# Issuing the value loads of a decode attention kernel from ScalarE's DMA queue

## The chip, the cores and the metric

The kernel runs on one core of one Trainium2 chip. A core has five engines that run their own instruction streams: TensorE (PE in the profile), VectorE (DVE), ScalarE (ACT), GpSimd (POOL) and SyncE (SP). Work moves between HBM and the on-chip memory on 16 DMA engines; SP and ScalarE each have a DMA queue of their own, which the profile calls q1 and q10. The metric is the device time of one execution in microseconds.

## The reference, cut to what matters

One token (a row of 448) goes through a block of grouped-query attention over a long cache and, beside it, a small mixer MLP; a gate mixes the two.

```python
q = x @ wq                                  # 16 query heads of 256
k, v = repeat(k_cache, 2), repeat(v_cache, 2)   # 8 heads x 65536 rows x 256, bf16
p = softmax(q k^T / 16)
a = (p v) @ wo
b = mixer_mlp(layernorm(x))                 # 448 x 1792, elementwise in S = 1
g = sigmoid(sum(x * gate_w))
out = g * a + (1 - g) * b
```

Nearly all of the work is reading the two caches once: 8 heads x 65536 rows x 256 values of two bytes, twice.

## The kernel before, in words

The cache is cut into 32 loads (NP) of keys and 32 of values, four of each (PPH) to a head. A load is 128 partitions x 128 rows (NV) of 256 bf16 values: 8 MB, of which each partition gets 64 KB in one piece. The 32 iterations follow the loads.

Keys live in a ring of 192 slots (`kring`), one and a half loads long. Values live in one buffer of 128 slots (`vbuf`), exactly one load: the next values can be fetched only when the last value matrix multiplication on the present ones has ended.

What each engine does in iteration j:

- TensorE (the loop from L531): `keys` transposes the eight chunks of key load j into PSUM (L355) and multiplies them with the queries (L376). Four chunks lie in the first half of the load, four in the second. Then `values` multiplies the probabilities with the values in `vbuf` (L407, 128 of them) and signals `sem_pv`. From iteration 3 on (LEAD is 2) the values lag the keys by one load: iteration j consumes key load j and value load j-1. At the start of the next iteration comes `maxima` (L393, L395), two small steps that VectorE needs for the running maximum of load j. At the end of a head (every fourth iteration) TensorE also projects the finished head (L457, L468).
- VectorE (the loop with `evacuate`, L675): copies half of the transposed chunks out of PSUM, computes the running maximum (`maxima`, L681 to L704), and in iterations 4 to 17 a step of the mixer MLP (`mixer`, L650 to L668), whose middle, a tanh, is on ScalarE.
- ScalarE (the loop with L820): copies the other half of the chunks, then `weights` computes the probabilities of this load (L803 and L807, after a wait for VectorE's maximum), and in iterations 4 to 17 (MIX0 is 4, 14 steps) the mixer's tanh (L825, after a wait for VectorE). Before its loop it issues six small loads (L780 to L785).
- SP (L256 to L319) does nothing but issue DMAs, in an order written out by hand, each behind the wait that makes its buffer free. Key load j goes out when the first half of load j-1 has been transposed (`sem_tr`); key loads 0, 2, 3 and 31 go out in halves or smaller parts. Behind it, after a wait on `sem_pv`, goes value load j-1 (`load_v`, L271 to L281), and at a head's end the next slice of the projection matrix `wo` (L259). The last value load, 31, goes out in five pieces after the loop, the first of them into the key ring.

All these loads stand in SP's one queue, so they are carried out in the order of issue.

Of the kernel before, what the change touches and what calls it, by code (L numbers as in the profile page):

```python
# [12 lines left out]
def bass_gated_mix__gqa_block_cached__mixer_token_mlp__decode_kernel(  # L13
# [25 lines left out]
    P = 128  # L39
# [11 lines left out]
    NV = BODY * NT  # L51
    NP = NC // BODY
    PPH = NCPH // BODY
# [9 lines left out]
    LEAD = 2  # L63
# [32 lines left out]
    with ctx:  # L96
        def sb(shape, dt, name):
            return ctx.enter_context(nc.sbuf_tensor(name, shape, dt))
# [4 lines left out]
        def new_sem(name):  # L103
            return ctx.enter_context(nc.semaphore(name))
# [3 lines left out]
        vbuf = sb([P, NV, DH], bf16, "vbuf")  # L108
# [91 lines left out]
        sem_v = new_sem("sem_v")  # L200
# [11 lines left out]
        sem_pv = new_sem("sem_pv")  # L212
# [8 lines left out]
        s_hb = new_sem("s_hb")  # L221
# [11 lines left out]
        s_q = new_sem("s_q")  # L233
# [16 lines left out]
        def src(cache, j, n0=0, n1=NV):  # L250
            g, m = divmod(j, PPH)
            s = cache[0, g, m * BODY * CH:(m + 1) * BODY * CH, :].rearrange("(p n) d -> p n d", p=P)
            return s[:, n0:n1, :].rearrange("p n d -> p (n d)")

        @block.sync
        def _(eng):  # L256
            def load_wo(g):
                w = A_wo[g * REP * DH:(g + 1) * REP * DH, :]
                eng.dma_start(wo_rows, w.rearrange("(p i) n -> p (i n)", i=2 * REP)).then_inc(sem_wo, 16)  # L259

            load_wo(0)
            eng.dma_start(wq_s.rearrange("p u n -> p (u n)"),
                          A_wq.rearrange("r n -> (r n)").rearrange("(p m) -> p m", p=P)).then_inc(sem_wq, 16)
            def load(dst, cache, j, n0, n1, at, sem):
                eng.dma_start(dst[:, at + n0:at + n1, :].rearrange("p n d -> p (n d)"), src(cache, j, n0, n1)
                              ).then_inc(sem, 16)

            load(kring, A_k_cache, 0, HV, NV, 0, sem_k)
            load(kring, A_k_cache, 0, 0, HV, 0, sem_kb)

            def load_v(j):  # L271
                if j == 0:
                    eng.wait_ge(s_q, 1)
                    eng.wait_ge(s_hb, 1)
                else:
                    eng.wait_ge(sem_pv, j)
                load(vbuf, A_v_cache, j, 0, NV, 0, sem_v)
                g, m = divmod(j, PPH)
                if m == 0 and 1 <= g < H - 1:
                    eng.wait_ge(s_proj, g)  # L280
                    load_wo(g)  # L281

            for j in range(NP):
                if j == LEAD + 1:
                    eng.wait_ge(sem_tr[NB - 1], BODY * LEAD)
                    load(kring, A_k_cache, j, HV, NV, HV, sem_kc[1])
                    eng.wait_ge(sem_tr[NB - 1], BODY * LEAD + DC // 2)
                    load(kring, A_k_cache, j, 0, HV // 2, HV, sem_kq[0])
                if j >= 1:
                    eng.wait_ge(sem_tr[NB - 1], BODY * (j - 1) + DC)  # L290
                if j == LEAD:
                    load(kring, A_k_cache, j, HV, NV, 0, sem_k)
                    load(kring, A_k_cache, j, 0, HV, 0, sem_kc[0])
                elif j == LEAD + 1:
                    load(kring, A_k_cache, j, HV // 2, HV, HV, sem_kq[1])
                elif j == NP - 1:
                    load(kring, A_k_cache, j, 0, HV, HV, sem_k)
                    load(kring, A_k_cache, j, HV, NV, HV, sem_kc[2])
                elif j >= 1:
                    load(kring, A_k_cache, j, 0, NV, HV * (j % 2), sem_k)  # L300
                if j < LEAD:
                    load_v(j)
                elif j > LEAD:
                    load_v(j - 1)


            for (n0, n1), sem in zip(pieces, sem_vp):
                if n0 == 0:
                    eng.wait_ge(sem_tr[NB - 1], BODY * (NP - 1) + DC)
                elif n0 == NRING:  # L310
                    eng.wait_ge(sem_pv, NP - 1)
                load(kring if n1 <= NRING else vbuf, A_v_cache, NP - 1, n0, n1, 0, sem)
            eng.wait_ge(s_proj, H - 1)
            for h in range(REP):
                w = A_wo[(HQ - REP + h) * DH:(HQ - REP + h + 1) * DH, :]
                eng.dma_start(wo_sb[:, h, :], w.rearrange("(p j) n -> p (j n)", j=2)).then_inc(sem_wl[h], 16)
            eng.wait_ge(s_fin, NCG)
            eng.dma_start(out_ap, out_row[:, :]).then_inc(sem_out, 16)
            eng.wait_ge(sem_out, 16)  # L319
# [16 lines left out]
        def _(pe):  # L336
# [95 lines left out]
            def piece_wait(n):  # L432
                for (n0, _), sem in zip(pieces, sem_vp):
                    if n == n0:
                        pe.wait_ge(sem, 16)
# [342 lines left out]
        @block.scalar  # L778
        def _(act):
            act.dma_start(xrow_b, x_row_ap).then_inc(sem_x, 16)  # L780
            act.dma_start(grow_b, gate_w.rearrange("(a n) -> a n", a=1)).then_inc(sem_misc, 16)
            for i, w in enumerate((B_w1.rearrange("a f -> (a f)"), B_b1, B_w2.rearrange("f a -> (f a)"))):
                act.dma_start(wrows_b[i * FT:(i + 1) * FT, :], w.rearrange("(k p) -> k p", p=P)
                              ).then_inc(sem_misc, 16)
            act.dma_start(b2_b[:, :], B_b2.rearrange("(a n) -> a n", a=1)).then_inc(sem_misc, 16)  # L785
            act.sem_inc(sem_exp, 1)
            for b in range(1, NB, 2):
                act.sem_inc(sem_ev[b], 1)
            act.wait_ge(s_d2a, 1)
            act.sqrt(statb[:, 3:4], statb[:, 2:3])  # L790
            act.activation(statb[:, 5:6], statb[:, 4:5], AF.Exp, scale=-1.0).then_inc(s_a2d, 1)

            act.wait_ge(s_q, 1)
            act.activation(qrow[:, 1, :], kst[:, 1, :], AF.Copy).then_inc(s_qc, 1)

            pt_reg = act.alloc_register("pt_reg")
            act.reg_mov(pt_reg, DC)
            mix_reg = act.alloc_register("mix_reg")
            act.reg_mov(mix_reg, 1)

            def weights(j1):
                act.wait_ge(s_mneg, j1)
                act.activation(fade[:, :], mdif[:, :], AF.Exp, scale=scale).then_inc(s_fade, 1)  # L803
                for half in range(2):
                    p0 = act.snap(pt_reg, min_val=0, max_val=DC)
                    for hh in range(REP):
                        ins = act.activation(pT[:, bass.ds(p0, DC), hh:2 * NT:REP],  # L807
                                             scores_all.rearrange("p (a r n hh) -> p a hh r n", a=2, r=DC, hh=REP)[:, half, hh],
                                             AF.Exp, bias=mneg[:, hh:hh + 1], scale=scale)
                    if half == 0:  # L810
                        act.reg_sub(pt_reg, DC, pt_reg)
                ins.then_inc(sem_exp, 1)

            with nc.Fori(0, NP, 1, engines=OrderedEngineSet([act.engine])) as j:
                c0 = act.snap(j * BODY, min_val=0, max_val=NC)
                for k in range(BODY):
                    act.wait_ge(sem_qk, c0 + (k + 1))
                    for b in range(1, NB, 2):
                        act.wait_ge(sem_tr[b], c0 + (k + 1))
                        act.activation(ktT[:, k % KTB, b, :], kst_b[:, b, :], AF.Copy).then_inc(sem_ev[b], 1)  # L820
                weights(act.snap(j + 1, min_val=1, max_val=NP))
                with act.If(j >= MIX0):
                    with act.If(j < MIX0 + FT):
                        act.wait_ge(s_u, act.snap(mix_reg, min_val=1, max_val=FT))
                        act.activation(z_b[:, :], z_b[:, :], AF.Tanh).then_inc(s_tanh, 1)  # L825
                        act.reg_add(mix_reg, mix_reg, 1)
            act.wait_ge(s_proj, H)
            for q in range(1, NCG, 2):
                act.activation(out_row[:, q * WG:(q + 1) * WG], prj[32 * q:32 * q + 1, 0:WG], AF.Copy
                               ).then_inc(s_fin, 1)  # L830
# [28 lines left out]
```

## Time and profile before

| | us |
|---|---|
| median of 3 runs | 1264.16 |
| lowest and highest run | 1264.0 and 1265.95 |
| span of the profiled execution | 1262.9 |
| TensorE busy | 964.6 |
| ScalarE busy | 544.5 |
| VectorE busy | 500.2 |

The profile is one execution on the chip. Its page gives the span, busy times by engine, the span in 40 slices, the DMA queues and the costliest groups of instructions. Further views come from the same trace: waits (who waited for whom), the chain of work that ended last, and timelines of one engine in a window. A row of a timeline is: start in us, duration in us, engine and line, operation, output and input with shapes, the number of instructions merged into the row, and in brackets how long the engine was idle before it and what released it. A q after an engine's name means its sequencer, which issues DMAs and is not counted as busy. A row of waits is: who waited for what, us in total, how often, the longest.

### The profile page before, as it was taken

Reading aid. Unit: us, or ns where it says so; the run is one execution under the profiler, and the core shown is the slowest. Engines: PE = TensorE matmul, PEld = TensorE weight load, DVE = VectorE, ACT = ScalarE, POOL = GpSimd, SP = SyncE. Lnnn points to the kernel's source line nnn. Section 1 sums busy time; section 2 is a strip of 40 time slices with the busy share of each in tenths; the row PEclk is TensorE's granted clock in tenths of the full one; section 3 lists DMA queues with packets and bytes.
Section 4 is the critical chain, followed back from the end, with each engine's and each line's share of the span. In section 5 each row is a group of like instructions: output and inputs, shape, how many; then the busy total and the mean of one; then the engine's idle time right before and its main releaser. Section 6 shows DMA issues by size and latency. Waiting matters only on the chain.

```text
span 1262.9 us, 39617 instructions
## 1 busy us (share of the span) xinstructions
PE 964.6 (76%) x17024; PEld 881.7 (70%) x17024; DVE 500.2 (40%) x1128; ACT 544.5 (43%) x692; POOL 0.9 (0%) x7
## 2 busy tenths in 40 slices
PE   4768877688777797767878678876679867698786
PEld 3667876678766687666777667776678756687674
DVE  4334434444544435444444433343333423334342
ACT  2444543345533445333554334443344533345451
POOL 0000000000000000000000000000000000000000
PEclk8779887888878888888987879888798878888897
DMA  9999999999999999999999999999999999999998
GB/s 417 431 421 426 449 432 432 430 432 444 432 434 430 434 432 432 432 434 436 436 434 428 439 432 432 432 440 432 434 432 434 428 440 436 434 432 434 423 438 365
DMA packets 12053, 544.35 MB, mean 431 GB/s; under 512 B 1417, under 2 KB 1676, under 8 KB 2828
## 3 DMA queue, kind: packets, MB, share of 16 engines
q1 hardware_dynamic: 11954, 544.22, 99.7%
q8 instruction: 6, 0.10, 0.0%
q10 hardware_dynamic: 90, 0.01, 0.0%
q14 instruction: 3, 0.02, 0.0%
HBM read 544.22 MB, written 0.00 MB: 431 GB/s over the span
## 4 chain that ended last, share of the span: by engine, by line
DMA 60%; PE 36%; issue 2%; DVE 2%; DVEq 0%; ACT 0%; SPq 0%
DMA kring<-in_A_k_cache_dram 57%; PE kst L355 26%; PE sps L376 6%; DMA vbuf<-in_A_v_cache_dram 3%; PE acc L407 3%; PE acc L457 0%; PE prj L468 0%; PE sps L395 0%; DVE ktT L675 0%; DVE accs L709 0%; PE acc L400 0%; ACT z_b L825 0%; PE sps L393 0%; DVE mrow L686 0%; DVE z_b L656 0%
## 5 line engine op out<-in xcount | busy, mean ns | idle before, releaser
L355 PE MATMUL kst<-ident,kring 128*128 128x128 f32 x4096 | 556.9, 296 | 189.5 <-DMA kring<-in_A_k_cache_dram 166.6
L820 ACT ACTIVATE ktT<-kst 128x1024 bf16<-128x1024 bf16 x512 | 498.6, 1021 | 338.7 <-PE kst L355 338.3
L355 PEld LDWEIGHTS kst<-ident,kring 128*128 128x128 f32 x4096 | 505.1, 154 | 198.6 <-issue 192.3
L675 DVE COPY ktT<-kst 128x1024 bf16<-128x1024 bf16 x512 | 353.9, 692 | 436.0 <-PE kst L355 410.4
L376 PEld LDWEIGHTS sps<-qcur,ktT 128*128 128x128 bf16 x8192 | 238.0, 97 | 2.6
L376 PE MATMUL sps<-qcur,ktT 128*128 128x2 bf16 x8192 | 236.6, 163 | 0.0
L407 PE MATMUL acc<-vbuf,pT 128*2 128x256 bf16 x4008 | 160.0, 335 | 6.5 <-DMA vbuf<-in_A_v_cache_dram 3.7
L407 PEld LDWEIGHTS acc<-vbuf,pT 128*2 128x2 bf16 x4008 | 110.8, 102 | 47.6 <-issue 4.4
L803 ACT ACTIVATE fade<-mdif 128x2 f32<-128x2 f32 x32 | 6.5, 203 | 302.1 <-DVE mdif L692 302.1
L686 DVE TENSOR_REDUCE mrow<-sps 2x1 f32<-2x128 f32 x32 | 8.9, 278 | 159.9 <-PE sps L393 159.9
L395 PEld LDWEIGHTS sps<-mdiag,mones 2*128 2x128 f32 x64 | 11.2, 217 | 28.0 <-DVE mdiag L688 28.0
L807 ACT ACTIVATE pT<-sps,mneg 128x64 f32 x128 | 30.4, 335 | 0.0
L395 PE MATMUL sps<-mdiag,mones 2*128 2x2 f32 x64 | 13.9, 285 | 21.3 <-DVE mdiag L688 21.3
L393 PE MATMUL sps<-ident,mcol 128*2 128x128 f32 x32 | 9.0, 282 | 27.3 <-issue 25.8
L825 ACT ACTIVATE z_b<-z_b 128x448 bf16<-128x448 bf16 x14 | 8.1, 576 | 48.1 <-DVE z_b L662 48.1
L400 PE MATMUL acc<-pT,ones_sq 128*128 128x32 bf16 x256 | 12.0, 182 | 21.9 <-issue 18.4
L709 DVE COPY accs<-acc 128x288 f32<-128x288 f32 x8 | 3.7, 458 | 62.4 <-PE acc L407 62.4
L393 PEld LDWEIGHTS sps<-ident,mcol 128*2 128x2 f32 x32 | 2.6, 80 | 36.2 <-issue 28.1
L681 DVE TENSOR_REDUCE mcol<-sps 128x2 f32<-128x256 f32 x32 | 13.5, 423 | 33.8 <-PE sps L376 33.8
L400 PEld LDWEIGHTS acc<-pT,ones_sq 128*128 128x128 bf16 x256 | 8.8, 99 | 26.0 <-issue 22.3
L704 DVE TENSOR_SCALAR acc<-acc,fader 128x256 f32<-128x256 f32 x32 | 15.8, 493 | 2.5
L497 PE MATMUL kst<-vbuf,xcol 128*64 128x512 bf16 x28 | 5.5, 571 | 8.8 <-DMA vbuf<-in_A_wq_dram 8.8
(111 smaller groups left out, 173.9 us busy)
## 6 DMA issues: line engine op xcount, KB each, us to landing
kring<-in_A_k_cache_dram SPq DMA_DIRECT2D x7, 4096.0 KB, 26.4
kring<-in_A_v_cache_dram SPq DMA_DIRECT2D x1, 4608.0 KB, 27.6
kring<-in_A_k_cache_dram SPq DMA_DIRECT2D x2, 2048.0 KB, 15.1
vbuf<-in_A_wq_dram SPq DMA_DIRECT2D x1, 3584.0 KB, 12.0
wo_sb<-in_A_wo_dram SPq DMA_DIRECT2D x7, 448.0 KB, 25.5
vbuf<-in_A_v_cache_dram SPq DMA_DIRECT2D x1, 1536.0 KB, 9.3
vbuf<-in_A_v_cache_dram SPq DMA_DIRECT2D x1, 1024.0 KB, 11.4
vbuf<-in_A_v_cache_dram SPq DMA_DIRECT2D x1, 768.0 KB, 12.8
```

Of the source, the lines that this page charges most:

```text
L355: ins = pe.transpose(kst[:, b, i * P:(i + 1) * P], kring_f[:, at + NT * (k % DC) + 4 * b + i, :], ident[:, :])
L376: ins = pe.matmul(sps[:, 0, 2 * (NT * k + nt):2 * (NT * k + nt) + 2], ktT[:, par, b, ntl * DH + dj:(ntl + 1) * DH:2], qcur[:, dj, :], star ...
L393: pe.transpose(mxT, mcol[:, :], ident[:, :]).then_inc(s_mT, 1)
L395: pe.matmul(mxB, mones[:, :], mdiag[:, :], start=True, stop=True).then_inc(s_mB, 1)
L400: pe.matmul(acc[:, DENC:SELC], ones_sq[:, :], pT[:, r, :], start=False, stop=(r == BODY - 1), skip_group_check=True)
L407: ins = pe.matmul(acc[o:o + REP, 0:DH], pT[:, r, 2 * nt:2 * nt + 2], buf[:, n, :], start=False, stop=False, skip_group_check=True)
L675: vec.tensor_copy(ktT[:, k % KTB, b, :], kst_b[:, b, :]).then_inc(sem_ev[b], 1)
L681: vec.tensor_reduce(out=mcol[:, :], in_=scores_all.rearrange("p (n hh) -> p hh n", hh=REP), axis=AX.X, op=ALU.max)
L686: vec.tensor_reduce(out=mrow[:, :], in_=mxT, axis=AX.X, op=ALU.max)
L704: vec.tensor_scalar(acc[:, 0:DENC], acc[:, 0:DENC], fader[:, :], None, op0=ALU.mult).then_inc(s_acc, 1)
L807: ins = act.activation(pT[:, bass.ds(p0, DC), hh:2 * NT:REP], scores_all.rearrange("p (a r n hh) -> p a hh r n", a=2, r=DC, hh=REP)[:, hal ...
L820: act.activation(ktT[:, k % KTB, b, :], kst_b[:, b, :], AF.Copy).then_inc(sem_ev[b], 1)
```

## The change

Value loads 0 to 30 are issued by ScalarE instead of SP. The first goes out ahead of ScalarE's loop, after a wait on `s_hb`; the others at the head of iterations 1, 2 and 4 to 31, ahead of the iteration's copies. The load's number is held in a register that counts up, and the wait on `sem_pv` and the source address in HBM follow the register. SP keeps all key loads, the loads of `wo` with their wait on `s_proj`, and the five pieces of value load 31. Buffers, sizes and semaphores stay as they are.

```diff
-            def load_v(j):
-                if j == 0:
-                    eng.wait_ge(s_q, 1)
-                    eng.wait_ge(s_hb, 1)
-                else:
-                    eng.wait_ge(sem_pv, j)
-                load(vbuf, A_v_cache, j, 0, NV, 0, sem_v)
+            def load_w(j):
                 g, m = divmod(j, PPH)
                 if m == 0 and 1 <= g < H - 1:
                     eng.wait_ge(s_proj, g)
...
                 if j < LEAD:
-                    load_v(j)
+                    load_w(j)
                 elif j > LEAD:
-                    load_v(j - 1)
+                    load_w(j - 1)
...
+            v_by_load = A_v_cache[0, :, :, :].rearrange("g (m p n) d -> (g m) p (n d)", m=PPH, p=P)
+            v_dst = vbuf[:, :, :].rearrange("p n d -> p (n d)")
+            act.wait_ge(s_hb, 1)
+            act.dma_start(v_dst, v_by_load[0, :, :]).then_inc(sem_v, 16)
+            i_reg = act.alloc_register("i_reg")
+            act.reg_mov(i_reg, 1)
             with nc.Fori(0, NP, 1, engines=OrderedEngineSet([act.engine])) as j:
                 c0 = act.snap(j * BODY, min_val=0, max_val=NC)
+                with act.If(j > 0):
+                    with act.If(j != LEAD + 1):
+                        i = act.snap(i_reg, min_val=1, max_val=NP - 2)
+                        act.wait_ge(sem_pv, i)
+                        act.dma_start(v_dst, v_by_load[bass.ds(i, 1), :, :].rearrange("o p n -> p (o n)")
+                                      ).then_inc(sem_v, 16)
+                        act.reg_add(i_reg, i_reg, 1)
                 for k in range(BODY):
                     act.wait_ge(sem_qk, c0 + (k + 1))
```

## The prediction

> **What bounds the kernel now.** I read the page first: span, DMA and queues.
>
> ```profile
> span 1262.9 us, 39617 instructions
> ...
> DMA  9999999999999999999999999999999999999998
> ...
> q1 hardware_dynamic: 11954, 544.22, 99.7%
> ...
> q10 hardware_dynamic: 90, 0.01, 0.0%
> ```
>
> The 16 DMA engines are busy in every slice, and q1, which only SyncE feeds, holds 99.7% of them. No edit that moves no bytes can win much; an edit that lets the engines run dry loses that time in full. So the question is when each load is put out, and the views of waits (TensorE's, then SP's) say what releases it.
>
> ```profile
> PE kst L355 <- DMA kring<-in_A_k_cache_dram: 166.6, 29, 9.1
> PE acc L407 <- DMA vbuf<-in_A_v_cache_dram: 3.7, 3, 2.5
> ```
> ```profile
> SPq L265 <- PE acc L407: 569.0, 30, 28.3
> ```
>
> TensorE waits for keys in nearly every iteration and almost never for values; SP puts a value load out as soon as the values pass (L407) that frees `vbuf` has ended. Now one iteration of the stretch in which the mixer runs (4 to 17), by the timelines of SP, TensorE, ScalarE and VectorE:
>
> ```profile
> 237.69 0.33 SPq L265 DMA_DIRECT2D vbuf<-in_A_v_cache_dram  x1
> 259.47 0.33 SPq L265 DMA_DIRECT2D kring<-in_A_k_cache_dram  x1
> 278.61 0.33 SPq L265 DMA_DIRECT2D vbuf<-in_A_v_cache_dram  x1
> ```
> ```profile
> 247.89 6.38 PE L355 MATMUL kst<-ident,kring 128*128 128x128 f32 x32 [8.05 <-DMA kring<-in_A_k_cache_dram]
> ...
> 273.23 5.33 PE L407 MATMUL acc<-vbuf,pT 128*2 128x256 bf16 x128
> ...
> 286.60 3.67 PE L355 MATMUL kst<-ident,kring 128*128 128x128 f32 x16 [5.81 <-DMA kring<-in_A_k_cache_dram]
> ```
> ```profile
> 281.09 0.20 ACT L803 ACTIVATE fade<-mdif 128x2 f32<-128x2 f32 x1 [9.55 <-DVE mdif L692]
> 281.21 0.95 ACT L807 ACTIVATE pT<-sps,mneg 128x64 f32 x4
> 285.58 0.58 ACT L825 ACTIVATE z_b<-z_b 128x448 bf16<-128x448 bf16 x1 [3.43 <-DVE z_b L662]
> ```
> ```profile
> 286.54 0.39 DVE L668 TENSOR_TENSOR gu<-wtmp,z_b 128x448 bf16<-128x448 bf16 x1
> ```
>
> Call 247.89 S, the start of an iteration's keys. The next keys are put out at S+11.6, the values pass starts at S+25.3 and ends at S+30.7, where the next values are put out; the next keys have landed at 286.60, S+38.7. In 38.7 us the engines move two loads of 8 MB, so one takes L = 19.35 us alone. The value load was queued 8.0 us (286.60 - 278.61) before the engines would have run dry. That is the kernel's slack.
>
> **The change, part by part.**
>
> *SP loses its waits on `sem_pv` but the last, and 31 issues* of 0.33 us. They held up nothing: each key load's own wait ended later (259.47 against 237.69). Worth 0. The wo loads keep their place.
>
> *ScalarE gains 31 issues,* at the head of its iteration. The added wait on `sem_pv` costs nothing: it is met when ScalarE arrives, since ScalarE first finishes the previous load's weights (L803, L807), which need the maxima TensorE computes after that same values pass. But there lies the price: the load is now put out after these weights and, in the 14 mixer iterations, after the tanh, which waits for VectorE. Against sem_pv at 278.61 the tanh starts 6.97 and ends 7.55 later; I take 7.3, as the sequencer may run ahead of the tanh or not. At a head's end the projection comes in between, and in later iterations there is no tanh:
>
> ```profile
> 199.90 0.33 SPq L265 DMA_DIRECT2D vbuf<-in_A_v_cache_dram  x1
> ...
> 210.40 0.58 ACT L825 ACTIVATE z_b<-z_b 128x448 bf16<-128x448 bf16 x1 [3.45 <-DVE z_b L662]
> ```
> ```profile
> 940.88 0.33 SPq L265 DMA_DIRECT2D vbuf<-in_A_v_cache_dram  x1
> ```
> ```profile
> 943.40 0.95 ACT L807 ACTIVATE pT<-sps,mneg 128x64 f32 x4
> ```
>
> There it is 10.50 against 6.97, so 3.5 more at a head's end, and 2.5 to 3.5 (I take 3.2) after the mixer. The issue itself, 0.33 us, lies in ScalarE's idle time.
>
> *Two queues instead of one.* The trace never has two big streams, but it has ScalarE's six small loads against SP's at the start:
>
> ```profile
> 0.73 0.53 ACTq L780 DMA_DIRECT2D vbuf<-in_A_x_dram  x1
> ...
> 2.85 0.32 ACTq L785 DMA_DIRECT2D b_b<-in_B_b_dram  x1
> ...
> 12.60 0.38 DVE L618 TENSOR_TENSOR vbuf<-vbuf 1x448 bf16<-1x448 bf16 x1 [4.00 <-DMA b_b<-in_B_b_dram]
> ```
> ```profile
> vbuf<-in_A_wq_dram SPq DMA_DIRECT2D x1, 3584.0 KB, 12.0
> wo_sb<-in_A_wo_dram SPq DMA_DIRECT2D x7, 448.0 KB, 25.5
> ```
> ```profile
> 1.66 21.21 DMA kring<-in_A_k_cache_dram
> ```
> ```profile
> SPq L319 <- DMA out_dram<-out_row: 0.8, 1, 0.8
> ```
>
> Two bytes put out at 2.85 arrived by 12.60. Behind SP's work in one line they would have come after the keys at 22.87; with precedence, in about the 1.1 us that the output took (0.3 of issue, 0.8 of wait). So the queues alternate. The 90 packets on q10 are three loads of 14 rows and three of one, each a data and a count packet (3x28 + 3x2). A DMA engine with a part in all six carries 12 in at most 11.9 us, 0.99 us each; one 28 KB packet of wq (3584 KB in 128 rows) at L's rate takes 19.35/8 x 28/64 = 1.06 us. That is one for one. Key and value loads both come in 64 KB rows, so half the rate each. The Trainium skill, "DMA: Bandwidth & Descriptors", section "Queues, rings and completion order", says the same, round robin per packet; the trace agrees (0.99 against 1.06 us).
>
> *What half and half does.* Take 1.0 us from issue to first byte (estimate: out_row's 1.1 us in all). Let the values' first byte come y after S. They run alone until the keys' first byte at S+12.6, have 19.35 - 12.6 + y = 6.75 + y left, now at half speed, and land at 12.6 + 2(6.75 + y) = 26.1 + 2y, instead of before S+19.35+y: sharing holds up the stream that is needed first. TensorE wants them at 25.3, so it waits 0.8 + 2y; sem_pv comes at 31.4 + 2y, the next values' first byte (7.3 + 1.0) at 39.7 + 2y, and the next keys land at 38.7 + y. So y' = y + 1.0: once the slack is gone, lateness grows by 1.0 us an iteration, and the DMA engines stand idle for y in each.
>
> It is capped. VectorE ends its mixer step at sem_pv + 8.3 (286.93 - 278.61), which is also the values' first byte, and it must then copy the next keys' first chunk before TensorE goes on:
>
> ```profile
> 211.36 0.39 DVE L668 TENSOR_TENSOR gu<-wtmp,z_b 128x448 bf16<-128x448 bf16 x1
> ...
> 212.77 1.97 PE L355 MATMUL kst<-ident,kring 128*128 128x128 f32 x16 [0.97 <-DVE ktT L675]
> ```
>
> That is 1.0 us after the step's end, where the second chunk otherwise starts at S+4.4 (6.38 - 1.95 for its 16 transposes; about 4.1 on the mean, an estimate). From y = 3.1 on, the keys' first half and with it the next key issue are later by y - 3.1, which leaves the values alone for longer: y settles where y - 3.1 = 1.0, at **4.1 us of idle DMA an iteration**. Four of the 14 late issues follow a head's end, with 3.5 more each.
>
> *The sum.* Mixer: 14 x 4.1 + 4 x 3.5 = 71.4; four wo loads of 1.06 us (448 of 8192 KB of L) fall into the holes, so 67. After the mixer growth is 1.0 - 4.1 = -3.1 an iteration: the lateness dies in one or two; the three heads left reach 3.2 + 3.5 + 1.0 = 7.7 of the 8.0, 0 to 4 each, I take 1: 3. Start: values 0 join the second half of keys 0, and values 2 go out at the end of iteration 1 and not in the middle of iteration 2, ahead of keys 3, whose parts have smaller rows and so get less than half; 0 to 9, I take 4. Tail: values 30 share with the first piece of values 31; 0 to 8, 1 as the pieces behind still fill the engines. 67 + 3 + 4 + 1 = 75: a span of 1337.9. The median of the runs is 1.3 over the span, so **1339 us**. The ends: 7.0 for 7.3, and a values pass of 4.6 for 5.33, bring growth to 0 (about -35); 1.5 of latency and 7.55 add 0.75 to growth and to y (about +10), with half a microsecond more of branch and register work another 7, and the start and tail add 12.
>
> **The rivals.**
>
> *Mild loss.* Growth is a small difference. With TensorE at full clock the values pass takes 3.66 us:
>
> ```profile
> 233.98 3.66 PE L407 MATMUL acc<-vbuf,pT 128*2 128x256 bf16 x128
> ```
>
> Growth is then -0.7, and only the head ends cost, some 3.5 + 2.8 + 2.1 + 1.4 = 10 per four iterations: 35 - 4 + 4, so about 1299. Against it: most rows stand near 5.3. Or the queues are served in order of issue: then 14 x 0.3 + 4 x 3.5 = 18, 1282; the b_b row speaks against it.
>
> *No change*, 1262 to 1266: the engines stay fed, and sharing only reorders loads. This needs the issue within about 6 us of sem_pv, where growth is below zero also at a head; the later stretch (3.2) has it, the mixer's 7.3 has not. The Trainium skill, same page, section "Issuing engines are not separate DMA queues", would give this: another issuing engine "will only save the time on the sequencer". It leaves out where in its program that engine stands.
>
> *Faster.* Place: the seam between loads. If two filled queues leave no gap between packets, the engines gain the 0.3% that q1 leaves (3.8 us), and with 1% more rate some 12: about 1250. It decides only where values are put out before the keys have landed, so if the delay stays under 7.0 (8.0 less 1.0 of latency).
>
> *Far worse.* If keys get 60%, values land at 12.6 + (6.75 + y)/0.4, y settles near 9 in the mixer (14 x 9 + 14) and no longer dies after it (about 60): some 1460. The one-for-one count speaks against it.
>
> **How the numbers follow.** The forecast (1300 to 1390) gets 0.72, mild loss 0.13, no change 0.06, faster 0.04, far worse 0.05. A difference under 0.2% can't be told from none here. Faster 0.04, same 0.06, slower 0.90. Range 1280 to 1390, with both kinds of mild loss inside.
>
> **What would show it.** Right: q10 carries about 260 MB; the GB/s row, 431 on the mean, drops to some 390 from slice 5 to 25 (38.7/42.8 of it) and returns; value issues on ScalarE 7 to 8 us after L407 ends in the mixer and 3 after it; TensorE's wait for `vbuf` at L407 rises from 3.7 us to 80 or more; iterations of about 43 us at 300 to 800 us, 39 after. Wrong: key and value loads that overlap and yet land at full speed each in order of issue; value issues under 6 us behind L407; a GB/s row that stays at 430; or a loss spread evenly over all iterations, which is the far worse case.

## The result, and the profile after

The changed kernel takes 1394.99 us (median of 4 runs, 1394.07 to 1399.52) against 1264.15: a ratio of 1.1041, 95% interval 1.1028 to 1.1054. The loss is 131 us where 75 were forecast, and the time lies above the range. The way in which it was lost is the one forecast; four sizes in the sum were off, those of the start and of the later heads badly.

The page of the changed kernel, its span, slices and queues:

```profile
span 1393.4 us, 39834 instructions
...
DMA  9979698998889888989889889999999999999996
GB/s 407 436 302 444 250 389 344 421 421 361 361 374 421 361 361 361 405 363 420 380 342 427 378 367 406 421 389 436 391 421 450 388 410 421 452 421 391 416 428 284
...
q1 hardware_dynamic: 7490, 284.17, 47.4%
q10 hardware_dynamic: 4554, 260.06, 44.3%
```

The bytes are the same, q10 now carries 260 MB of them, and the DMA engines are no longer full. The waits for loads, by the view of waits:

```profile
PEld acc L401 <- DMA vbuf<-in_A_v_cache_dram: 133.6, 20, 9.2
PE acc L401 <- DMA vbuf<-in_A_v_cache_dram: 131.5, 20, 9.0
...
PE kst L349 <- DMA kring<-in_A_k_cache_dram: 84.4, 26, 9.0
```

TensorE waited 3.7 us for values before and 131.5 now (L401 was L407), up to 9.0 us at a time; its wait for keys fell from 166.6 to 84.4. One mixer iteration by the timelines of TensorE and ScalarE:

```profile
501.12 3.61 PE L349 MATMUL kst<-ident,kring 128*128 128x128 f32 x16 [2.39 <-DMA kring<-in_A_k_cache_dram]
...
535.72 5.13 PE L401 MATMUL acc<-vbuf,pT 128*2 128x256 bf16 x128 [8.49 <-DMA vbuf<-in_A_v_cache_dram]
...
545.47 3.59 PE L349 MATMUL kst<-ident,kring 128*128 128x128 f32 x16 [2.41 <-DMA kring<-in_A_k_cache_dram]
```
```profile
543.36 0.20 ACT L797 ACTIVATE fade<-mdif 128x2 f32<-128x2 f32 x1 [17.84 <-DVE mdif L686]
...
547.85 0.58 ACT L832 ACTIVATE z_b<-z_b 128x448 bf16<-128x448 bf16 x1 [3.43 <-DVE z_b L656]
548.60 0.34 ACTq L820 DMA_DIRECT2D vbuf<-in_A_v_cache_dram  x1
```

The values pass ends at 540.85 (535.72 + 5.13), the next values go out at 548.60, 7.7 us later and 3.1 us after the next keys have begun. The iteration lasts 44.35 us (545.47 - 501.12) in place of 38.7, and the values pass starts 34.6 us into it in place of 25.3.

That the two queues share evenly is seen in a window with both streams, 517 to 532 us, in the view of DMA queues (packets, MB, share of the 16 engines):

```profile
q10 hardware_dynamic: 48, 3.15, 48.4%
q1 hardware_dynamic: 48, 3.15, 48.4%
```

Where the time went, by stretches: the starts of the keys of iterations 4, 19 and 31 cut the run into start, mixer, later part and tail. Before:

```profile
169.43 0.90 PE L355 MATMUL kst<-ident,kring 128*128 128x128 f32 x3 [4.62 <-DMA kring<-in_A_k_cache_dram]
```
```profile
754.20 3.03 PE L355 MATMUL kst<-ident,kring 128*128 128x128 f32 x13 [5.79 <-DMA kring<-in_A_k_cache_dram]
```
```profile
1213.45 1.96 PE L355 MATMUL kst<-ident,kring 128*128 128x128 f32 x16
```

After:

```profile
192.06 1.96 PE L349 MATMUL kst<-ident,kring 128*128 128x128 f32 x16 [0.70 <-DMA kring<-in_A_k_cache_dram]
```
```profile
856.23 2.18 PE L349 MATMUL kst<-ident,kring 128*128 128x128 f32 x9 [2.46 <-DMA kring<-in_A_k_cache_dram]
```
```profile
1335.07 1.96 PE L349 MATMUL kst<-ident,kring 128*128 128x128 f32 x16
```

So the start lost 22.6 us (192.06 - 169.43), the mixer 79.4 (664.17 against 584.77), the later part 19.6 (478.84 against 459.25) and the tail 8.9 (1393.4 - 1335.07 against 1262.9 - 1213.45). Together 130.5, the difference of the spans. The table cuts the experiments the same way, each from its one profiled execution.

| us more than before | start | mixer | later | tail |
|---|---|---|---|---|
| forecast | 4 | 67 | 3 | 1 |
| changed kernel | 22.6 | 79.4 | 19.6 | 8.9 |
| prompt issue (`e_early`) | 20.1 | 5.6 | 4.5 | 3.3 |
| late, one queue (`e_sp_late`) | 0.1 | 25.1 | 3.9 | -0.2 |
| ahead of the tanh (`e_before_tanh`) | 19.7 | 23.2 | 13.1 | 7.6 |
| loads 0 to 2 on SP (`e_start_sp`) | 0.4 | 67.4 | 19.2 | 4.2 |

### The profile page after: what moved, and what is told of

Its sections match the earlier page's. It is cut to its first block, busy times and chain, and to the rows that moved or that the text cites. A ratio compares the mean times of both kernels' runs of the same rounds, so it can differ in the third digit from the quotient of the medians.

```text
span 1393.4 us, 39834 instructions
## 1 busy us (share of the span) xinstructions
PE 992.9 (71%) x17024; PEld 897.7 (64%) x17024; DVE 499.4 (36%) x1128; ACT 545.5 (39%) x692; POOL 0.9 (0%) x7
## 4 chain that ended last, share of the span: by engine, by line
DMA 56%; PE 32%; DVE 5%; issue 4%; DVEq 1%; ACTq 0%; ACT 0%; SPq 0%; POOLq 0%
DMA vbuf<-in_A_v_cache_dram 35%; DMA kring<-in_A_k_cache_dram 21%; PE kst L349 15%; PE acc L401 10%; PE sps L370 4%; PE sps L389 1%; PE acc L451 1%; PE sps L387 0%; DVE mrow L680 0%; DVE z_b L650 0%; DVE wtmp L648 0%; DVE z_b L654 0%; DVE mdiag L682 0%; DVE wtmp L644 0%; DVE u_b L646 0%
## 5 line engine op out<-in xcount | busy, mean ns | idle before, releaser
L349 PE MATMUL kst<-ident,kring 128*128 128x128 f32 x4096 | 573.4, 301 | 167.3 <-DMA kring<-in_A_k_cache_dram 84.4
L349 PEld LDWEIGHTS kst<-ident,kring 128*128 128x128 f32 x4096 | 516.4, 156 | 179.0 <-issue 147.2
L401 PE MATMUL acc<-vbuf,pT 128*2 128x256 bf16 x4008 | 172.0, 352 | 131.5 <-DMA vbuf<-in_A_v_cache_dram 131.5
L401 PEld LDWEIGHTS acc<-vbuf,pT 128*2 128x2 bf16 x4008 | 113.7, 107 | 183.1 <-DMA vbuf<-in_A_v_cache_dram 133.6
L451 PEld LDWEIGHTS acc<-sel,accs 128*64 128x64 f32 x112 | 10.8, 214 | 0.9
## 6 DMA issues: line engine op xcount, KB each, us to landing
vbuf<-in_A_wq_dram SPq DMA_DIRECT2D x1, 3584.0 KB, 11.6
```

The source lines that it names most:

```text
L349: ins = pe.transpose(kst[:, b, i * P:(i + 1) * P], kring_f[:, at + NT * (k % DC) + 4 * b + i, :], ident[:, :])
L401: ins = pe.matmul(acc[o:o + REP, 0:DH], pT[:, r, 2 * nt:2 * nt + 2], buf[:, n, :], start=False, stop=False, skip_group_check=True)
L451: ins = pe.matmul(dst[hh * HP:(hh + 1) * HP, i:i + 1], accs[:, i:DH:2 * REP], sel[:, hh:hh + 1], start=False, stop=True, skip_group_check= ...
```

## The experiments

Theory A is the prediction's: the late issue uses up the slack, and sharing by halves turns each late microsecond into more. Rival B: sharing costs by itself. Rival C: the delay alone explains it. The edits are cut to their main lines.

**Prompt issue from ScalarE (`e_early`).** Sharing without delay: `next_v` waits on `sem_pv` and issues the load. The wait stops nothing there, since the weights need maxima that come after the same values pass.

```diff
+                with act.If(j > LEAD):
+                    with act.If(j < NP - 1):
+                        next_v()
                 weights(act.snap(j + 1, min_val=1, max_val=NP))
```

> Value loads 3 to 30 still come from ScalarE's queue, but are issued as soon as the values pass has ended: the wait on sem_pv stands ahead of the weights instead of behind the weights and the tanh. Loads 0 to 2 as in the changed kernel. Theory A (a late issue, made worse by sharing): with the delay gone the middle of the run is back at 38.7 us an iteration and only the start (about 22 us) and the tail (up to 9) remain lost: 1280 to 1297 us. Rival B (sharing the DMA engines between two queues costs by itself, as the stream that is needed first runs at half rate): no change against the changed kernel, 1380 to 1400. Rival C (only the delay matters, the start and tail too): 1264 to 1270.

Measured: 1298.57 us (1296.58 to 1300.74), ratio 1.0273 (1.0256 to 1.029), 1.6 us above A's range and far from those of B and C. Its windows from the start of keys 4 on, in the view by windows (window, length, busy time of the engines, granted clock, DMA share, GB/s):

```profile
190.00:780.00 590.00, 452.53 (x7973) 415.60 (x7970) 254.41 (x596) 258.49 (x331) 0.00 (x0) 0.85 1.00 432
```

Against the changed kernel's:

```profile
192.00:856.00 664.00, 468.87 (x7973) 423.55 (x7973) 254.30 (x599) 258.88 (x333) 0.00 (x0) 0.81 0.90 382
```

With the delay gone the engines are full again at 432 GB/s, though both streams still share. B falls for the middle of the run; for the start it holds (20.1 us). C falls, as the start's loss has no delay in it: value loads 1 and 2 went out 0.2 us behind the end of their values passes.

**Late issue on one queue (`e_sp_late`).** Delay without sharing: SP issues as before, but waits for a count that ScalarE raises at the place of its issue.

```diff
                     eng.wait_ge(sem_pv, j)
+                    eng.wait_ge(s_go, j)
                 load(vbuf, A_v_cache, j, 0, NV, 0, sem_v)
```

> The kernel before with its one queue, but SP issues a value load only when ScalarE has come to the point at which it would issue it in the changed kernel. Delay without sharing. Theory A: the values land one transfer after the late issue and keys are not held up, so an iteration loses only what the delay is over the slack: about 1.4 us in the ten plain mixer iterations, about 4 at the four mixer head ends, nothing later: 1285 to 1295 us. Rival B: nothing is shared, so 1264 to 1268. Rival C (the delay alone explains the loss): 1380 to 1400.

Measured: 1293.94 us (1292.67 to 1296.9), ratio 1.0241 (1.0224 to 1.0258), as A said. TensorE hardly waits for values, by the view of waits:

```profile
PE kst L357 <- DMA kring<-in_A_k_cache_dram: 196.1, 29, 13.8
...
PE acc L409 <- DMA vbuf<-in_A_v_cache_dram: 4.4, 3, 2.2
```

The same delay that makes TensorE wait 131.5 us for values when keys share the engines makes it wait 4.4 here, as on one queue a value load, once begun, is not held up by keys; the loss shows in the wait for keys instead (196.1 against 166.6). Delay alone costs 29.7 us (1293.94 - 1264.28), sharing alone 34.3, of which 20.1 at the start, both together 131: about 67 us belong to neither alone. In the mixer stretch they are 25.1, 5.6 and 79.4, so 48.7 of it belong to neither.

**Issue between weights and tanh (`e_before_tanh`).** A shorter delay, forecast at 4.0 us, and 7.4 at a head's end.

```diff
                 weights(act.snap(j + 1, min_val=1, max_val=NP))
+                with act.If(j > LEAD):
+                    with act.If(j < NP - 1):
+                        next_v()
                 with act.If(j >= MIX0):
```

> As the changed kernel, but from iteration 3 on the issue stands between the weights and the tanh: 4.0 us behind the end of the values pass instead of 7.7, and 7.4 instead of 11.2 at a head's end. Theory A: lateness then shrinks by some 2 us an iteration outside head ends, so only start, tail and head ends cost: 1295 to 1325 us. Rival B: as the changed kernel, 1380 to 1400. Rival C: in proportion to the delay, so about half of the loss: 1325 to 1340.

Measured: 1320.11 us (1312.44 and 1327.78), ratio 1.0441 (1.037 to 1.0511). The mean is in A's range, but of the two runs one lies in A's range and one in C's. The delay came out at 3.3 to 3.4 us, and 6.6 to 6.9 at a head's end; a plain iteration by the timelines of TensorE and ScalarE (499.51 + 3.66 to 506.51):

```profile
499.51 3.66 PE L401 MATMUL acc<-vbuf,pT 128*2 128x256 bf16 x128
```
```profile
506.51 0.34 ACTq L818 DMA_DIRECT2D vbuf<-in_A_v_cache_dram  x1
```

The whole loss, 55.8 us of 131, would fit a proportion to the delay (3.3 of 7.7) too, so the stretches decide: in the profiled run, the slower of the two, the mixer stretch falls from 79.4 to 23.2, under a third. That is less than in proportion, on the trace of one run.

**Loads 0 to 2 on SP (`e_start_sp`).** The start alone.

```diff
+                if j <= LEAD:
+                    load(vbuf, A_v_cache, j, 0, NV, 0, sem_v)
```

> As the changed kernel, but value loads 0 to 2 stay on SP's queue at their old places. It measures the start alone. All theories: if the start costs what the two traces show there, 22.6 us up to the keys of iteration 4, this gives it back: 1367 to 1377 us. If the lost time at the start would have been lost later anyway: 1385 to 1395.

Measured: 1361.15 us (1355.38 and 1366.92), ratio 1.0765 (1.0712 to 1.0819). The start's loss is gone (0.4), and the time fell by more than it, to below the range: in the profiled execution, with a span of 1354.1, the mixer lost 67.4 instead of 79.4. The last section comes back to this.

**Keys in halves (`e_k_halves`)** and **values in halves (`e_v_halves`)**: do the engines share by packets or by bytes? Each load of 64 KB rows becomes two of 32 KB rows in the same queue.

```diff
-                    load(kring, A_k_cache, j, 0, NV, HV * (j % 2), sem_k)
+                    load(kring, A_k_cache, j, 0, HV, HV * (j % 2), sem_kh)
+                    load(kring, A_k_cache, j, HV, NV, HV * (j % 2), sem_k)
```

> The changed kernel with key loads 4 to 30 put out as two halves, one behind the other, so that their rows are 32 KB and the values' still 64 KB. If the DMA engines take one packet from each queue in turn, values now get two thirds while both streams are there, land earlier, and lateness grows more slowly: 1325 to 1365 us. If the engines share by bytes: 1385 to 1400, as the changed kernel.

> The changed kernel with every value load put out as two halves, one behind the other, so that the values' rows are 32 KB and the keys' 64 KB. In turn by packets, values get one third while both are there, so every iteration waits for them and the lateness feeds itself even where the issue is only 4 us late: 1550 to 1700 us. By bytes: 1385 to 1405.

Measured: keys in halves 1329.21 and 1354.38 us in two runs; values in halves 1603.93 us (1597.73 and 1610.14), ratio 1.2686 (1.263 to 1.2743). The waits for values, keys in halves first:

```profile
PE acc L411 <- DMA vbuf<-in_A_v_cache_dram: 35.5, 13, 4.9
```
```profile
PE acc L402 <- DMA vbuf<-in_A_v_cache_dram: 384.4, 29, 18.6
```

Same bytes, same places of issue, and 35.5 (in the longer of its two runs) or 384.4 us of waiting, to either side of the changed kernel's 131.5: the share goes by packets. A window of the second with both streams, 418 to 429 us, shows it directly, as many packets from each queue and half the bytes from q10:

```profile
q1 hardware_dynamic: 48, 3.15, 66.0%
q10 hardware_dynamic: 48, 1.57, 33.1%
```

This kernel is the prediction's "far worse" rival come true: with a third of the rate the lateness no longer dies after the mixer.

**What is left (`e_early_start`, `e_early_ends`, `e_ends_wo`).** The prompt issue with loads 0 to 2 on SP; with load 30 on SP as well; and with the later loads of `wo` moved from SP's queue to ScalarE's.

```diff
+                if j <= LEAD or j == NP - 2:
+                    load(vbuf, A_v_cache, j, 0, NV, 0, sem_v)
```

> The kernel with the prompt issue on ScalarE (ahead of the weights), and value loads 0 to 2 back on SP at their old places. Theory A: nothing is left but the tail (3 us) and what sharing itself still costs in the middle, 5.6 and 4.5 us by the trace of the kernel with the prompt issue alone: 1268 to 1279 us. If the two queues cost nothing beside delay and start: 1264 to 1267.

> As the one with loads 0 to 2 on SP and a prompt issue, with value load 30 on SP as well, so that the tail is that of the kernel before. If the 3 us of the tail come from load 30 sharing with the first piece of load 31, this is 3 us faster than that kernel: 1265 to 1276 us. Faster than the kernel before by more than 0.2% only if two queues move more bytes a second than one, which no trace here shows so far.

> The kernel with the prompt issue and value loads 0 to 2 and 30 on SP, with the six later loads of wo moved from SP's queue to ScalarE's, at the head of iterations 5, 9 to 25, where they stand behind the head's first value load and no longer ahead of key loads. In the traces of the prompt kernels iterations behind a head's end take up to 42 to 44 us in place of 38.7 and the next ones less, since eight small wo packets ahead of the keys each wait for a 64 KB value packet. If that is what is left of the loss in the middle (6.3 and 2.7 us): 1264 to 1268 us. If the two queues cost by themselves: 1269 to 1274, as without the move.

Measured: 1278.32 us (1275.83 to 1289.59), ratio 1.0101 (1.0084 to 1.0118); 1271.72 us (1270.0 to 1273.78), ratio 1.0054 (1.0037 to 1.0071); and with `wo` moved 1282.82 us (1273.6 to 1296.86), ratio 1.0123 (1.0083 to 1.0162) by its three faster runs. The start and the tail account for most of what the prompt kernel lost: with their loads back on SP 7.4 of its 34.3 us are left. The guess about `wo` fell: the runs of that kernel lie between 1273.6 and 1296.86 us, above both of its ranges on the median, so the move did not help; why it hurt is open.

No kernel with value loads on ScalarE's queue reached the kernel before. Of the 9.6 us by which the span of `e_early_ends` is longer (1272.5 against 1262.9), 7.0 are packets that took longer for the same bytes: by its page q1 and q10 hold 58.2% and 41.3% of the span, 1266.1 us, against 99.7% of 1262.9, 1259.1. Why they took longer there is open.

## Why the prediction was wrong, point by point

- *What bounds the kernel* was right: the DMA engines, and a slack of 8.0 us. So was "SP's waits are worth 0": no trace shows a gain from taking them away.
- *The delay of the issue* was 7.3 in the mixer and 3.2 after it; measured 7.7 and 4.0, and 7.4 to 7.5 at the later heads' ends. The issue comes 0.17 us after the tanh's end (548.60 against 547.85 + 0.58 = 548.43), so ScalarE's sequencer does not run ahead of it here. After the mixer, one late values pass, by the timelines of TensorE and ScalarE:

```profile
1047.39 5.30 PE L401 MATMUL acc<-vbuf,pT 128*2 128x256 bf16 x128
```
```profile
1056.68 0.35 ACTq L820 DMA_DIRECT2D vbuf<-in_A_v_cache_dram  x1
```

- *Half and half* was right, and by packets: 48 to 48 in the window, and both experiments with halves. The Trainium skill, "DMA: Bandwidth & Descriptors", section "Queues, rings and completion order", has this rule; by these runs it decides the time. Of when the values land the working missed two things that nearly cancel. The keys issued at 513.03 had no packet before 517.7, some 4.7 us later in place of 1.0: first each engine took two more packets of values. And the 16 small packets that close the load came only after 534.7, though the last of the values' data was through at 532.9: one more packet of keys came in between on each engine. By the view of DMA queues, 513.03 to 517.7 and 534.7 to 535.5 us:

```profile
q10 hardware_dynamic: 32, 2.10, 103.8%
```
```profile
q10 hardware_dynamic: 16, 0.00, 1.1%
```

  So the values pass began 34.6 us into the iteration, close to the 26.1 + 2 x 4.1 = 34.3 of the formula by luck.
- *Lateness that feeds itself* was right. Kernels with either half of the cause lose 5.6 and 25.1 us in the mixer stretch, the one with both 79.4.
- *The mixer's sum*, 67 us of idle engines against 79.4 lost, was short by a term that it had at nothing. The queues' shares of the mixer stretch (192.06 to 856.23 us, and before 169.43 to 754.2):

```profile
q10 hardware_dynamic: 2160, 125.83, 45.3%
q1 hardware_dynamic: 2736, 127.67, 44.5%
```
```profile
q1 hardware_dynamic: 4893, 253.30, 100.1%
```

  The engines were busy for 596.4 us of 664.17 (89.8%) and idle for 67.8; before, they were busy for 585.4, all the time. The other 11.0 us are packets that took longer for the same bytes: when the engines start again after running dry, the first packet on each takes 2.97 us (247.6% of 1.2 us, the window from 505 to 506.2) where 19.35/8 = 2.42 is usual.

```profile
q10 hardware_dynamic: 16, 1.05, 247.6%
```

  That the idle time came out within 1 us is in part luck. In the plain iteration shown above (501.12 to 545.47) the engines are idle for 5.05 us (11.4% of 44.35) and not for 4.1; after two of the head ends they are idle for less (last section).

```profile
q10 hardware_dynamic: 144, 8.39, 44.9%
q1 hardware_dynamic: 144, 8.39, 43.7%
```
- *The start* was the step that failed most, the term of the sum "0 to 9, I take 4": it measured 22.6. Value load 0 shares with the second half of key load 0; the windows of the first iterations:

```profile
23.00:80.00 57.00, 35.62 (x525) 32.59 (x526) 13.44 (x27) 17.01 (x21) 0.00 (x0) 0.67 0.85 364
80.00:159.00 79.00, 50.07 (x910) 46.97 (x908) 26.89 (x54) 33.05 (x42) 0.00 (x0) 0.85 0.97 418
159.00:192.00 33.00, 29.24 (x523) 26.92 (x523) 12.65 (x25) 15.96 (x19) 0.00 (x0) 0.88 0.61 254
```

  In the first, the engines are idle for 15% of 57 us, 8.6 us; in the third, iteration 3, for 39% of 33 us, 12.9. The prediction named the cause, small rows of key load 3 against 64 KB rows of values 2, but did not follow it to the end. Iteration 3 begins with the half of load 3 that comes in two quarters, issued last, with rows of 16 KB, and GpSimd gives the sign for them:

```profile
159.17 5.71 PE L349 MATMUL kst<-ident,kring 128*128 128x128 f32 x32 [9.82 <-POOLq L327]
```
```profile
170.08 0.33 SPq L265 DMA_DIRECT2D kring<-in_A_k_cache_dram  x1
```

  They came at 159.17 where iteration 3 began at 131.82 before; the next keys need half of these keys done, so they went out at 170.08, and with values 2 long landed nothing was left to move. `e_start_sp` shows that it is these loads.
- *The later heads*, "0 to 4 each, I take 1", was mis-sized next: 19.6 in all with the end of the mixer's lateness. The engines run dry around each head's end and are full between, by windows:

```profile
930.00:985.00 55.00, 39.94 (x616) 35.15 (x609) 18.66 (x48) 19.41 (x28) 0.00 (x0) 0.75 0.90 375
985.00:1095.00 110.00, 84.71 (x1556) 78.03 (x1556) 37.87 (x75) 47.30 (x57) 0.00 (x0) 0.86 1.01 436
1095.00:1145.00 50.00, 35.57 (x564) 32.40 (x563) 17.54 (x43) 18.93 (x28) 0.00 (x0) 0.81 0.92 387
```

  That is 5.5 us (10% of 55) and 4.0 us (8% of 50) of idle engines at two of the three, before what the longer packets add. With two queues the loss of this part goes with the delay: 4.5 us at 0.2 (`e_early`), 13.1 at 3.4 (`e_before_tanh`), 19.6 at 4.0. That a delay of 4.0 in place of 3.2 lets lateness shrink more slowly and leaves no slack at a head's end fits, but was not tried by itself.
- *The tail*, 1 against 8.9: values 30 go out at the head of iteration 31 and share with the first piece of values 31; the pieces behind wait for the pass on values 30, which in turn waited 5.5 us for its values:

```profile
1371.16 5.54 PE L401 MATMUL acc<-vbuf,pT 128*2 128x256 bf16 x128 [5.49 <-DMA vbuf<-in_A_v_cache_dram]
```

- *The rivals.* No change and faster: refuted, since the delay of 7.7 us is above the 6 and 7 that they needed. Mild loss: refuted by the size of the loss, and the queues do not serve in order of issue. Far worse: not this kernel, but real, as `e_v_halves` shows.
- *The range* ended at 1390. Its upper end left 12 us for start and tail, which took 26.5 more than the sum had (31.5 against 5), and the later part 16.6 more; these errors had one sign, not several.

## What to carry to other kernels

In these runs a second DMA queue on a full set of DMA engines added no rate (432 GB/s in the middle of the prompt kernel, 433 before); it took rate from the stream that was needed first, in shares set by the packet sizes of the two queues. Before moving a load to a computing engine's queue, ask what stands in that engine's program between the event that frees the buffer and the issue, and compare it with the time by which the load is queued ahead today. If it must move, put the issue at the earliest point at which its wait is met, and do not let loads with small rows share the engines with one of large rows.

## What the runs showed of the hardware that was not expected

At two head ends of the mixer stretch TensorE ran its transposes at half speed for over 12 us, though it was busy all that time. The first of them, by TensorE's timeline and the view by windows:

```profile
242.80 3.68 PE L349 MATMUL kst<-ident,kring 128*128 128x128 f32 x16 [3.91 <-DVE ktT L669]
...
256.60 1.96 PE L349 MATMUL kst<-ident,kring 128*128 128x128 f32 x16 [0.62 <-issue]
```
```profile
242.80:255.00 12.20, 12.20 (x113) 12.02 (x114) 4.65 (x7) 6.03 (x6) 0.00 (x0) 0.50 0.86 371
```

The chunk takes 3.68 us in place of 1.96, and the granted clock of the window is 0.50; what lowered it is open. In this kernel that need not be a loss: slow transposes put off the next key issue and leave the engines to the late values for longer. SP's timeline has it at 255.20, 19.6 us after the keys began (235.56) in place of 11.6:

```profile
255.20 0.33 SPq L265 DMA_DIRECT2D kring<-in_A_k_cache_dram  x1
```

The iteration behind it stands idle for 2.1 us (the two queues hold 48.3% and 46.6% of 243.5 to 285 us) against 5.05 in the plain one. `e_start_sp` has a mean clock of 0.78 over its mixer stretch against 0.81 and loses less there (67.4 against 79.4). That fits, but was not tried by itself.

The packets' time grew too: 91.7% of 1393.4 us (q1 and q10) is 1278 us against 1259 (99.7% of 1262.9) for the same bytes, 1.5% more. By the trace's packets, 378 of 64 KB that began when most engines stood idle took 3.10 us on the mean, the others 2.42: that is 16 of the 19 us, and so the price of running dry is more than the dry time. In the prompt kernel, 97.6% of 1296.5, it is 1265.
